# A Fourier layer and two gated blocks in one kernel: bias product on 128 rows, deferred threshold passes, and a later first inverse block

## The chip, the cores and the metric

The kernel runs on one core of one Trainium2 chip. The metric is the device time of one execution in microseconds (us). Three executions of the kernel before gave 1218.69, 1220.3 and 1221.24 us, median 1220.3. The engines are called PE (TensorE, the matrix engine), VectorE (DVE in the rows), ScalarE (ACT), GpSimd (POOL) and SyncE (SP, which only issues DMAs here). Each takes its own instructions in the order of the program and waits for the others by semaphores.

## What is computed

`x` has the shape 2 x 3008 x 256. The reference first applies a layer in the frequency domain, then two gated blocks on all 6016 tokens:

```python
X = np.fft.rfft(x, axis=1)
Yr = Xr @ w_r - Xi @ w_i + b_r
Yi = Xr @ w_i + Xi @ w_r + b_i
Yr = np.sign(Yr) * np.maximum(np.abs(Yr) - lam, 0.0)     # lam = 0.01, the same for Yi
y = np.fft.irfft(Yr + 1j * Yi, n=x.shape[1], axis=1)
h = y @ w_in;  x1 = (h * np.clip(h + 3.0, 0.0, 6.0) / 6.0) @ w_out       # d_ff 2048
out = (silu(x1 @ w_gate) * (x1 @ w_val)) @ w2_out                       # d_ff 1536
```

## The kernel before

**Layout of the transform.** 3008 is 47 x 64. The forward transform is done in two stages of matmuls, the inverse likewise. Frequencies are handled in 12 groups: 2 batches times 6 (`ORDER`, line 468), here called group 0 to 11. `pre` (line 309) is stage one on a slice of the input; its results go through DRAM (`Bd`) and come back transposed as `z`. Per group p:

- `s2` (line 384), stage two, called for two halves of the features. Eight PE matmul records each (L391). ScalarE copies one part of the result (L397) and rounds all of it to the high part of `X` (L398); VectorE forms a third combination, `sum` (L399), and the low part of `X` (L130). High and low part of the sum follow: a ScalarE cast (L404) and a VectorE subtraction (L130), both through the lists `later` and `last`.
- `ln` (line 421), the learned product with the complex weights in split precision, called for two halves h of the frequencies. One matmul of `ones` with `shift` adds the biases (L438): both tiles have 64 rows, of which rows 0 and 32 of `ones` are 1 and carry the high and the low part of the bias. 18 products follow (L433 to L435): 12 into bank `p`, on top of the bias, and 6 into bank `p1`. ScalarE copies `p1` (`k1`, L444), VectorE adds it to both halves of `p` (`yb`, L446), ScalarE takes a relu (`yc`, L448), VectorE a min and an addition (`yp`, L450): the last two are the threshold.
- `ia` (line 452), the first stage of the inverse: 16 PE records on half of the rows each (64 rows, `tile_position` 0 or 64, L459), two ScalarE copies (L462), and a DMA from GpSimd's queue to `Cd` in DRAM (L463).

`post` (line 544) is the second stage of the inverse for one block of 512 tokens and one half of the features: it needs `ct`, which `load_ct` (line 528) reads back from `Cd`, does 12 PE records (L541), a ScalarE cast to the high part `xa` (L552) and a VectorE subtraction for the low part (L130). The first block needs the groups 0 to 5 of batch 0 complete.

`unit` (line 618) is one step of the first gated block on the first tokens: one or two steps of weight conversion (`conv1.step`, line 197: four VectorE and two ScalarE instructions and a load `st`), `lower` (line 583, the split of the previous unit's result: a cast L579 and a subtraction L130), `project1` (line 555: six products, L125 to L127, then a relu L563 and a min and product L564), and `outp` (six products for each of two outputs). From group 8 on (`FROM`), units run between the pieces of the groups, and the last 4 groups thus share PE with them. Conversion steps run in `ln` for the groups 1 to 7.

**Order.** The order is written out by hand in the list `seq` (lines 488 to 504); each entry is called through `run` (line 411). For group p, `l` is the two halves of `ln`, `S(p + 1)` the two halves of the next group's stage two, `a` the inverse of the group before, `u` a unit from group 8 on:

```python
seq += l[:1] + u + some + S(p + 1)[:1] + u + S(p + 1)[1:] + a + u + l[1:] + u
seq += [sent]
...
if p == NQ:
    seq += [lambda: nc.sync.dma_start(inv2_sb, inv2), lambda: load_ct(blocks[0])]
if p == FROM - 1:
    seq += [lambda: few.__setitem__(0, True)]
    seq += [lambda: post(blocks[0], 0), lambda: post(blocks[0], 1)]
```

So `post` for the first block is issued between group 7 and group 8, and the load of its `ct` behind group 6. `run` puts the high sums of the step before ahead of a step and their low parts behind it. Two or three PSUM pools serve the matmuls: eight banks in turn up to group 7, five from then on (`few`). The tag `r` has three buffers, which `yb`, `yc` and the units' results share.

Behind the groups the remaining units, the first gated block and the second one follow (line 640 on); the diff does not touch them, except for the list that `run` and `unit` empty.

`prepare` (line 262) fills `ones` on GpSimd (L272 to L275) and the biases on VectorE and ScalarE (L291 to L294) while stage one runs.

Of the kernel before, what the change touches and what calls it, by code (L numbers as in the profile page):

```python
# [83 lines left out]
def fourier_moe_kernel(ctx: ExitStack, tc: tile.TileContext, x, lin, bias, w1, w2, fwd1, inv2, fwd2,  # L84
# [44 lines left out]
    def low(o, full, hi):  # L129
        nc.vector.tensor_tensor(out=o, in0=full, in1=hi.bitcast(F32), op=ALU.subtract)  # L130
# [92 lines left out]
    shift = ap_.tile([64, 2 * DIM], F32R, name="shift")  # L223
    ones = ap_.tile([64, 128], F32R, name="ones")
# [37 lines left out]
    def prepare():  # L262
# [8 lines left out]
        o = spread("o_st")[:64, :128]  # L271
# [3 lines left out]
        nc.gpsimd.tensor_copy(ones, o)  # L275
        w = [lin_st[:, k] for k in range(2)]
# [11 lines left out]
        def shifts(i):  # L288
            b = b_st[:64]
            if i == 0:  # L290
                nc.vector.tensor_scalar(b, b, LAM, None, op0=ALU.add)  # L291
                nc.scalar.copy(shift, b)
            else:
                low(shift[32:], b[32:], shift[32:])  # L294
# [8 lines left out]
    def spread(name):  # L303
        return xs_p.tile([128, 2 * DIM], F32, tag="r", name=name, bufs=3)
# [79 lines left out]
    def s2(b, Q, dh):  # L384
# [18 lines left out]
        def then():  # L403
            nc.scalar.copy(hi_s, both_)  # L404
            last.append(lambda: low(lo_s, both_, hi_s))
# [3 lines left out]
    later, last = [], []  # L409

    def run(f):

        for g in later:
            g()
        later.clear()
        f()
        for g in last:
            g()
        last.clear()

    def ln(b, Q, h):
# [3 lines left out]
        if 0 < ORDER.index((b, Q)) < FROM:  # L425
            conv1.step()
        xs = [t[:, :, :, h * 128 : (h + 1) * 128] for t in X[b, Q]]
# [20 lines left out]
        nc.scalar.activation(yc, yb, AF.Relu, bias=edges)  # L448
        yp[b, Q, h] = ap_.tile([128, 2, DIM], F32, tag="yp", name=f"yp{b}_{Q}_{h}", bufs=3)
        nc.vector.scalar_tensor_tensor(out=yp[b, Q, h], in0=yb, scalar=0.0, in1=yc, op0=ALU.min, op1=ALU.add)  # L450
# [40 lines left out]
    for p in range(len(ORDER)):  # L491
# [3 lines left out]
        seq += l[:1] + u + some + S(p + 1)[:1] + u + S(p + 1)[1:] + a + u + l[1:] + u  # L495
# [5 lines left out]
        if p == FROM - 1:  # L501
            seq += [lambda: few.__setitem__(0, True)]
            seq += [lambda: post(blocks[0], 0), lambda: post(blocks[0], 1)]
# [114 lines left out]
    def unit():  # L618
# [7 lines left out]
        if 0 <= n - 1 < len(units):  # L626
            lower(units[n - 1])
        if n < len(units):
            k, f = units[n]
            state[units[n]] = project1(k, f, ntok(k))  # L630
# [568 lines left out]
```

## Time and profile before

| | |
|---|---|
| median of three executions | 1220.3 us (1218.69 to 1221.24) |
| the profiled execution | 1220.05 us, span 1218.3 us |
| PE busy | 1204.9 us, 99% of the span |
| PE weight loads busy (beside the matmuls) | 1000.6 us, 82% |
| VectorE, ScalarE, GpSimd busy | 919.0 us (75%), 777.4 us (64%), 49.7 us (4%) |
| mean granted clock of PE | 0.996 of full speed |
| instructions | 16275 |

The page divides the span into 40 slices of 30.5 us and gives the busy share of each engine and the clock granted to PE in tenths. The ends of matmuls in the trace are modelled, so matmuls overlap in it, and an interval is best measured from start to start. An idle time with "<-" behind it names what ended it. A line number is that of the kernel; L130 is the helper that forms every low part, so its rows are told apart by tile names.

### The profile page before, as it was taken

Reading aid. Unit: us, or ns where it says so; the run is one execution under the profiler, and the core shown is the slowest. Engines: PE = TensorE matmul, PEld = TensorE weight load, DVE = VectorE, ACT = ScalarE, POOL = GpSimd, SP = SyncE. Lnnn points to the kernel's source line nnn. Section 1 sums busy time; section 2 is a strip of 40 time slices with the busy share of each in tenths; the row PEclk is TensorE's granted clock in tenths of the full one; section 3 lists DMA queues with packets and bytes.
Section 4 is the critical chain, followed back from the end, with each engine's and each line's share of the span. In section 5 each row is a group of like instructions: output and inputs, shape, how many; then the busy total and the mean of one; then the engine's idle time right before and its main releaser. Section 6 shows DMA issues by size and latency. Waiting matters only on the chain.

```text
span 1218.3 us, 16275 instructions
## 1 busy us (share of the span) xinstructions
PE 1204.9 (99%) x5770; PEld 1000.6 (82%) x5770; DVE 919.0 (75%) x1631; ACT 777.4 (64%) x1431; POOL 49.7 (4%) x77
## 2 busy tenths in 40 slices
PE   9998999999999999999999999999999999999998
PEld 3788787888888888888889888888888888888997
DVE  5676876798888988998988766766666766766665
ACT  3565665677777777777767655655655665655554
POOL 3000000800000000000000000000000000000000
PEclk9998999999999999999999999999999999999999
DMA  8875541774454563464362544644644644644551
GB/s 299 298 266 185 175 136 61 243 259 156 165 195 153 169 217 132 149 228 147 121 238 108 182 156 155 225 156 156 225 158 159 227 163 164 228 161 158 190 194 70
DMA packets 58450, 220.12 MB, mean 181 GB/s; under 512 B 5968, under 2 KB 17584, under 8 KB 46640
## 3 DMA queue, kind: packets, MB, share of 16 engines
q1 hardware_dynamic: 55728, 209.92, 49.3%
q0 software_dynamic: 2496, 9.05, 2.2%
q8 instruction: 45, 0.74, 0.2%
q14 instruction: 37, 0.30, 0.1%
q10 hardware_dynamic: 144, 0.11, 0.0%
HBM read 172.66 MB, written 46.40 MB: 180 GB/s over the span
## 4 chain that ended last, share of the span: by engine, by line
PE 88%; DVE 5%; ACT 2%; DMA 2%; issue 2%; SPq 0%; POOL 0%; DVEq 0%; ACTq 0%; POOLq 0%
PE acc L127 11%; PE acc L125 11%; PE acc L126 11%; PE P L901 8%; PE P L903 8%; PE P L902 8%; PE Tb L902 4%; PE Tb L901 4%; PE Tb L903 4%; PE p L541 3%; PE Q L902 2%; PE Q L901 2%; PE Q L903 2%; PE p L459 1%; PE p L324 1%
## 5 line engine op out<-in xcount | busy, mean ns | idle before, releaser
L957 ACT COPY hold<-P 128x512 f32<-128x512 f32 (+1 forms) x224 | 128.3, 573 | 77.0 <-PE P L903 76.9
L130 DVE TENSOR_TENSOR gated<-s,gated 128x512 fp32r<-128x512 f32 (+1 forms) x144 | 97.3, 676 | 50.2 <-ACT gated L1086 50.2
L579 ACT CAST gated<-r 128x512 fp32r<-128x512 f32 (+1 forms) x160 | 98.1, 613 | 54.7 <-DVE r L948 54.6
L130 DVE TENSOR_TENSOR gated<-r,gated 128x512 fp32r<-128x512 f32 (+1 forms) x160 | 107.8, 674 | 22.3 <-ACT gated L579 18.4
L952 DVE TENSOR_TENSOR hold<-Q,hold 128x512 f32<-128x512 f32 (+1 forms) x112 | 75.9, 678 | 64.5 <-PE Q L903 53.8
L125 PE MATMUL acc<-gated,w_o 128*128 128x512 f32 (+1 forms) x320 | 124.5, 389 | 0.0
L127 PE MATMUL acc<-gated,w_o 128*128 128x512 f32 (+1 forms) x320 | 123.2, 385 | 0.0
L126 PE MATMUL acc<-gated,w_o 128*128 128x512 f32 (+1 forms) x320 | 123.2, 385 | 0.0
L944 ACT ACTIVATE r<-hold,consts 128x512 f32<-128x512 f32 (+1 forms) x120 | 85.7, 714 | 40.9 <-DVE hold L952 40.0
L127 PE MATMUL acc<-gated,slot 128*128 128x512 f32 (+1 forms) x288 | 111.1, 386 | 0.0
L125 PE MATMUL acc<-gated,slot 128*128 128x512 f32 (+1 forms) x288 | 111.0, 385 | 0.1
L126 PE MATMUL acc<-gated,slot 128*128 128x512 f32 (+1 forms) x288 | 110.9, 385 | 0.0
L952 DVE TENSOR_TENSOR hold<-P,hold 128x512 f32<-128x512 f32 (+1 forms) x112 | 75.8, 677 | 40.0 <-PE P L903 40.0
L1126 ACT ACTIVATE s<-hold 128x512 f32<-128x512 f32 (+1 forms) x72 | 44.8, 623 | 85.6 <-DVE hold L952 85.6
L952 DVE TENSOR_TENSOR hold<-Tb,hold 128x512 f32<-128x512 f32 (+1 forms) x112 | 76.0, 678 | 25.8 <-PE Tb L903 18.8
L901 PE MATMUL P<-xo,slot 128*128 128x512 f32 (+1 forms) x240 | 92.3, 385 | 1.8 <-DVE hold L952 1.2
L903 PE MATMUL P<-xo,slot 128*128 128x512 f32 (+1 forms) x240 | 91.6, 382 | 0.0
L902 PE MATMUL P<-xo,slot 128*128 128x512 f32 (+1 forms) x240 | 91.5, 381 | 0.0
L948 DVE SCALAR_TENSOR_TENSOR r<-r,hold 128x512 f32<-128x512 f32 (+1 forms) x120 | 81.2, 677 | 13.3 <-ACT r L944 12.2
L1086 ACT CAST gated<-s 128x512 fp32r<-128x512 f32 (+1 forms) x144 | 88.0, 611 | 1.2 <-DVE s L1141 1.2
L1131 ACT ACTIVATE s<-hold 128x512 f32<-128x512 f32 (+1 forms) x72 | 45.0, 625 | 51.9 <-DVE hold L952 50.2
L127 PEld LDWEIGHTS acc<-gated,w_o 128*128 128x128 f32 x320 | 60.1, 188 | 11.3
(189 smaller groups left out, 2914.8 us busy)
## 6 DMA issues: line engine op xcount, KB each, us to landing
slot<-Wd SPq DMA_DIRECT2D x72, 1152.0 KB, 5.1
slot<-Sd SPq DMA_DIRECT2D x40, 896.0 KB, 4.8
st<-in_w SPq DMA_DIRECT2D x68, 256.0 KB, 4.9
Wd<-slot SPq DMA_DIRECT2D x12, 1152.0 KB, 5.1
z<-Bd SPq DMA_DIRECT2D x12, 512.0 KB, 5.3
Cd<-cs POOLq DMA_DIRECT2D x12, 512.0 KB, 4.7
Xd<-x SPq DMA_DIRECT2D x20, 256.0 KB, 2.3
raw<-Xd SPq DMA_DIRECT2D x5, 1024.0 KB, 7.4
```

The costliest lines, as they stand in the source:

```text
L125: nc.tensor.matmul(o, wl, xh, start=start, stop=False)
L126: nc.tensor.matmul(o, wh, xh, start=False, stop=False)
L127: nc.tensor.matmul(o, wh, xl, start=False, stop=stop)
L130: nc.vector.tensor_tensor(out=o, in0=full, in1=hi.bitcast(F32), op=ALU.subtract)
L579: nc.scalar.copy(hi[:, :n], g[:, :n])
L901: nc.tensor.matmul(o, wl, x[m][:, 0, :n], start=start, stop=False, skip_group_check=not start)
L902: nc.tensor.matmul(o, wh, x[m][:, 1, :n], start=False, stop=False, skip_group_check=not start)
L903: nc.tensor.matmul(o, wh, x[m][:, 0, :n], start=False, stop=True, skip_group_check=not start)
L944: nc.scalar.activation(r[:, :n], x[:, :n], AF.Relu, bias=three)
L952: nc.vector.tensor_tensor(out=h, in0=x[:, :n], in1=c, op=ALU.add)
L957: nc.scalar.copy(c, x[:, :n])
L1086: nc.scalar.copy(hi[:, :nb], t[:, :nb])
```

## The change

Four edits:

- `shift` and `ones` get 128 rows. The rows of `ones` but 0 and 32 stay zero, and rows 64 to 127 of `shift` are zeroed by a copy on GpSimd. The bias product thus runs on all 128 rows; the inverse (`ia`) keeps its 64-row form.
- `then` of `s2` issues the cast of the sum and the low part together. `ln` puts its relu and min into `later` as well. `run` hands the closures of the step before to `due`, and `flush` empties that list: behind the step, or inside it, in `ln` ahead of the products and in `unit` behind `lower`.
- `post` of the first block moves from the end of group 7 to behind the first half of `ln` of group 8, ahead of its first unit.
- In group 6 (`p == NQ`) the order becomes first half of `ln`, first half of stage two, inverse of group 5, second half of stage two, second half of `ln`.

```diff
@@ -220,8 +220,8 @@
     ap_ = pool(attn_stack, "attn", "right")
     linh = ap_.tile([128, 3, 2, DIM], F32R, name="linh")
     linl = ap_.tile([128, 3, 2, DIM], F32R, name="linl")
-    shift = ap_.tile([64, 2 * DIM], F32R, name="shift")
-    ones = ap_.tile([64, 128], F32R, name="ones")
+    shift = ap_.tile([128, 2 * DIM], F32R, name="shift")
+    ones = ap_.tile([128, 128], F32R, name="ones")
 
     NT = NJ // 4
     TC = 4 * DIM
@@ -268,11 +268,12 @@
             nc.gpsimd.memset(room[5][:, h * TC : (h + 1) * TC], 0.0)
         load_x(5)
         load_m(0, 0)
-        o = spread("o_st")[:64, :128]
+        o = spread("o_st")[:, :128]
         nc.gpsimd.memset(o, 0.0)
         for r in (0, 32):
             nc.gpsimd.memset(o[r : r + 1], 1.0)
         nc.gpsimd.tensor_copy(ones, o)
+        nc.gpsimd.tensor_copy(shift[64:], zeros[64:])
         w = [lin_st[:, k] for k in range(2)]
 
         def mixed(op):
@@ -289,9 +290,9 @@
             b = b_st[:64]
             if i == 0:
                 nc.vector.tensor_scalar(b, b, LAM, None, op0=ALU.add)
-                nc.scalar.copy(shift, b)
+                nc.scalar.copy(shift[:64], b)
             else:
-                low(shift[32:], b[32:], shift[32:])
+                low(shift[32:64], b[32:], shift[32:64])
 
         amid.update({
             6: [lambda: mixed(ALU.subtract), lambda: hi(2, 0)], 7: [lambda: mixed(ALU.add), lambda: hi(0, 2)],
@@ -402,21 +403,22 @@
 
         def then():
             nc.scalar.copy(hi_s, both_)
-            last.append(lambda: low(lo_s, both_, hi_s))
+            low(lo_s, both_, hi_s)
 
         later.append(then)
 
-    later, last = [], []
+    later, due = [], []
+
+    def flush():
+        while due:
+            due.pop(0)()
 
     def run(f):
 
-        for g in later:
-            g()
+        due.extend(later)
         later.clear()
         f()
-        for g in last:
-            g()
-        last.clear()
+        flush()
 
     def ln(b, Q, h):
 
@@ -424,6 +426,7 @@
             n_t[b, Q] = table("n", inv1, Q, f"n{b}_{Q}", 3)
         if 0 < ORDER.index((b, Q)) < FROM:
             conv1.step()
+        flush()
         xs = [t[:, :, :, h * 128 : (h + 1) * 128] for t in X[b, Q]]
 
         def product(o, form, k, start):
@@ -445,9 +448,13 @@
         yb = xs_p.tile([128, 2, DIM], F32, tag="r", name=f"yb{b}_{Q}_{h}", bufs=3)
         nc.vector.tensor_tensor(out=yb, in0=p, in1=k1.unsqueeze(1).to_broadcast([128, 2, DIM]), op=ALU.add)
         yc = xs_p.tile([128, 2, DIM], F32, tag="r", name=f"yc{b}_{Q}_{h}", bufs=3)
-        nc.scalar.activation(yc, yb, AF.Relu, bias=edges)
-        yp[b, Q, h] = ap_.tile([128, 2, DIM], F32, tag="yp", name=f"yp{b}_{Q}_{h}", bufs=3)
-        nc.vector.scalar_tensor_tensor(out=yp[b, Q, h], in0=yb, scalar=0.0, in1=yc, op0=ALU.min, op1=ALU.add)
+        y = yp[b, Q, h] = ap_.tile([128, 2, DIM], F32, tag="yp", name=f"yp{b}_{Q}_{h}", bufs=3)
+
+        def then():
+            nc.scalar.activation(yc, yb, AF.Relu, bias=edges)
+            nc.vector.scalar_tensor_tensor(out=y, in0=yb, scalar=0.0, in1=yc, op0=ALU.min, op1=ALU.add)
+
+        later.append(then)
 
     def ia(b, Q):
         c4 = ring4(f"cs{b}_{Q}")
@@ -492,7 +499,12 @@
         l, a = L(p), A(p - 1)
         some = [rest.pop(0) for _ in range(p in (1, 2))]
         u = [lambda: unit()] if p >= FROM else []
-        seq += l[:1] + u + some + S(p + 1)[:1] + u + S(p + 1)[1:] + a + u + l[1:] + u
+        head = l[:1] + ([lambda: post(blocks[0], 0), lambda: post(blocks[0], 1)] if p == FROM else [])
+        s = S(p + 1)
+        if p == NQ:
+            seq += head + s[:1] + a + s[1:] + l[1:]
+        else:
+            seq += head + u + some + s[:1] + u + s[1:] + a + u + l[1:] + u
         seq += [sent]
         if p in (2, 3):
             seq += [lambda i=p - 2: write_second(i)]
@@ -500,7 +512,6 @@
             seq += [lambda: nc.sync.dma_start(inv2_sb, inv2), lambda: load_ct(blocks[0])]
         if p == FROM - 1:
             seq += [lambda: few.__setitem__(0, True)]
-            seq += [lambda: post(blocks[0], 0), lambda: post(blocks[0], 1)]
     seq += [lambda: unit()] + A(len(ORDER) - 1)
 
 
@@ -625,6 +636,7 @@
                 conv1.step()
         if 0 <= n - 1 < len(units):
             lower(units[n - 1])
+        flush()
         if n < len(units):
             k, f = units[n]
             state[units[n]] = project1(k, f, ntok(k))
```

## Rows read from the trace of the kernel before

**Rows 1.** The page, busy tenths in 40 slices: PE and its granted clock.
```profile
PE   9998999999999999999999999999999999999998
PEclk9998999999999999999999999999999999999999
```
**Rows 2.** Stretches: length, busy us (count) by engine, granted clock, DMA share, GB/s.
```profile
63.07:65.75 2.68, 2.68 (x21) 2.44 (x21) 1.38 (x3) 1.42 (x3) 0.70 (x2) 1.00 0.77 231
91.12:101.10 9.98, 9.74 (x74) 8.34 (x72) 7.71 (x19) 6.54 (x17) 0.75 (x1) 1.00 0.59 188
99.46:103.07 3.61, 3.06 (x20) 2.55 (x20) 2.98 (x9) 3.11 (x9) 0.60 (x1) 1.00 0.03 9
108.00:112.35 4.35, 1.52 (x13) 1.34 (x12) 3.66 (x9) 3.37 (x10) 0.00 (x0) 0.94 0.86 227
117.60:122.20 4.60, 4.60 (x20) 4.17 (x20) 0.69 (x1) 0.58 (x1) 0.00 (x0) 0.52 0.07 27
```
**Rows 3.** Timeline of PE, groups 0 to 7: start, duration, instruction, idle before.
```profile
43.02 0.28 PE L434 MATMUL p<-linh,X 128*128 128x256 f32 x1
44.00 0.39 PE L435 MATMUL p<-linh,X 128*128 128x256 f32 x1 [0.70 <-DVE X L130]
...
45.94 1.95 PE L391 MATMUL p<-m,z 128*128 128x128 f32 x16
...
58.58 2.00 PE L459 MATMUL p<-yp,n 64*128 64x256 f32 x16
60.22 0.57 PE L438 MATMUL p<-shift,ones 64*128 64x512 f32 x1
...
60.95 0.28 PE L434 MATMUL p<-linh,X 128*128 128x256 f32 x1
...
62.86 0.28 PE L435 MATMUL p<-linh,X 128*128 128x256 f32 x1
...
63.72 0.28 PE L434 MATMUL p<-linh,X 128*128 128x256 f32 x1
63.84 0.28 PE L435 MATMUL p<-linh,X 128*128 128x256 f32 x1
...
94.96 2.00 PE L459 MATMUL p<-yp,n 64*128 64x256 f32 x16
...
112.35 5.32 PE L541 MATMUL p<-inv_sb,ct 96*128 96x94 f32 x24 [2.83 <-DMA ct<-Cd]
```
**Rows 4.** Timeline of PE: an inverse with full-row products behind it (group 9).
```profile
148.97 2.00 PE L459 MATMUL p<-yp,n 64*128 64x256 f32 x16
150.90 0.50 PE L125 MATMUL ph<-xa,w_g 128*128 128x512 f32 x1
151.24 0.40 PE L126 MATMUL ph<-xa,w_g 128*128 128x512 f32 x1
151.48 0.40 PE L127 MATMUL ph<-xa,w_g 128*128 128x512 f32 x1
```
**Rows 5.** Timelines of VectorE and of ScalarE in group 6.
```profile
97.93 0.69 DVE L450 SCALAR_TENSOR_TENSOR yp<-yb,yc 128x512 f32<-128x512 f32 x1 [0.79 <-ACT yc L448]
...
101.10 1.07 ACT L462 COPY cs<-p 128x512 f32<-128x512 f32 x2
```
**Rows 6.** Timeline of PE, groups 8 to 11.
```profile
128.05 1.99 PE L459 MATMUL p<-yp,n 64*128 64x256 f32 x14 [0.51 <-DVE r L564]
...
159.31 1.46 PE L541 MATMUL p<-inv_sb,ct 96*128 96x52 f32 x12
...
190.64 0.50 PE L125 MATMUL acc<-gs,w_o 128*128 128x512 f32 x1 [0.72 <-ACT gs L579]
```
**Rows 7.** Timelines of GpSimd and SP; the page's DMA issues, last number median landing.
```profile
14.73 0.51 POOL L331 DMA_DIRECT2D Bd<-first  x1 [4.47 <-DVE first L328]
...
38.72 0.38 SPq L380 DMA_DIRECT2D z<-Bd  x1
...
z<-Bd SPq DMA_DIRECT2D x12, 512.0 KB, 5.3
```

## Prediction

> **What bounds the kernel now.** I read the 40 slices of the page first. TensorE (PE) is at 90% or more in nearly every slice, and its clock has one dip behind the start, in the fourth slice [rows 1]. So the time is PE's work, plus the moments in which PE stands, plus what the lower clock costs. The diff reorders only the first 210 us; what follows keeps its instructions and their order and should move as a block.
>
> The table of stretches [rows 2] compares one piece of work. The 19 matmuls of the first half of `ln` (the bias product L438, then 18 products) take 2.68 us in group 3, 3.61 in group 7, and 4.60 in group 8, where the granted clock is 0.52, the lower of the two levels (1.2 GHz) nearly throughout. From 108.00 to 112.35 PE is busy for 1.52 us of 4.35. PE's timeline says why: it waits 0.70 us for `X` at 44.00, and 2.83 us for the transfer of `ct` at 112.35 [rows 3].
>
> VectorE and ScalarE cause both. In group 6 they need 9.98 us from one inverse's copies to the next, VectorE busy for 7.71 of it [rows 2], while PE's own pitch is 9.1 us (58.58 to 94.96, four groups, [rows 3]). VectorE's idle part stands above all in front of L450, 0.79 us each time, waiting for the relu issued just ahead of it [rows 5]. They fall nearly 0.9 us behind per group: the inverse of group 5 starts on PE at 94.96 [rows 3], its copies on ScalarE only at 101.10 [rows 5], 6.14 us later. The way from these copies through Cd and `ct` to L541 ends at 112.35, another 11.25 us.
>
> **The bias product on 128 rows.** From the last full-row product (62.86) to the second product behind the bias (63.72) is 0.86 us [rows 3]. With full rows I expect the pitches of ordinary neighbours: 0.12 (63.72 to 63.84), then 0.24 for 512 columns (151.24 to 151.48, [rows 4]), then 0.12: 0.48. Saved: 0.38. That holds for 17 of the 24 products: 12 first halves, and the second halves of groups 0 and 8 to 11, which no inverse precedes directly. 17 x 0.38 = 6.5 us.
>
> The second halves of groups 1 to 7 come behind the half-row inverse (in group 6 half of stage two now lies between; I count it alike). Before, from the first inverse matmul to the second product: 58.58 to 60.95 = 2.37 us [rows 3]. After, the switch of row modes lies ahead of the bias, as it does ahead of L125: 148.97 to 151.24 = 2.27 [rows 4], plus 0.12 = 2.39. So 7 x 0.02 = 0.1 is lost. The Trainium skill (TensorE: Matmul & The Clock Gate, Why this matters for your kernels) speaks against the change here: matmuls of few rows on different row groups run at the same time, and few rows take no less time than many. By that rule alone these seven lose their overlap with the inverse, 0.29 us each (L438 starts 1.64 us behind the first inverse matmul, L125 1.93), and the sum is 2 us smaller; the rows show the 0.29 come back at the exit. Between 0.1 and 2.0 I take 0.1, since both ends of it are measured.
>
> Group 0's first half gains little, since stage two behind it wants a `z` that lands about then: 0.1 off. The product's sum: **6.3 us**. The larger `ones` and the zeroing of 64 x 512 run on GpSimd, which is idle for 4.47 us ahead of its next DMA [rows 7]: 0 on the path, and above nothing only if they took longer than that, when the first Bd write would start as much later.
>
> **Threshold and sum passes a step later.** In a first half the relu and min now come behind stage two's first half, and the sums' high and low parts go together one step later. No instruction is added and no DMA moves with them. The stall ahead of L450 goes in first halves. Up to group 7 second halves keep it, because `sent` follows and flushes at once; and the last low sum now waits for the inverse's copies ahead of it on ScalarE (an estimate of 0.6, from two copies of 1.07 together, [rows 5]). VectorE's group becomes at most 7.7 + 0.8 + 0.6 = 9.1 us, PE's 9.1 - 0.4 = 8.7. It falls behind by 0.2 to 0.4 a group, 1 to 2 us by group 7. Two waits for `X` go: 43.02 to 44.00 in group 0, 0.98 - 0.12 = 0.86 [rows 3], and 3.61 - 2.68 = 0.93 in group 7 [rows 2]. **1.8 us.** What is late next is `z` of group 2: issued at 38.72 and landing 5.3 us later, at 44.0 [rows 7]; its stage two stands at 45.94 [rows 3] and moves up by 1.7. It just fits.
>
> In groups 8 to 11 the split of the previous unit now comes ahead of the relu and min. PE stood there 0.51 us for `r` at 128.05 and 0.72 for `gs` at 190.64 [rows 6]; by starts some 0.16 more each (0.86 against 0.70 at 44.00), so 1.5, and there may be shorter breaks which the view does not mark. The passes take 0.79 + 0.69 = 1.5 us out of the way [rows 5], more than either. I take **2.0** (0 to 3). `yp` comes later by some 3 us, but the inverse that reads it is a group behind.
>
> **First block a group later, inverse of group 5 earlier.** Nothing is added: 24 matmuls, two casts and two subtractions move behind the first half of group 8. The `ct` load keeps its place on SP; the tables, `st` and `z` queued behind it go out earlier with it. In group 6 the second half of stage two (half of 1.95 us, [rows 3]) moves behind the inverse, which so starts at about 94.96 - 1.0 - 3.5 (seven savings of 0.38 and the 0.86) = 90.5. With a lag of 1.5 to 3 us in place of 6.14 its copies begin by 93.5, and 11.25 later, by 104.8, `ct` is there. PE wants it at 109.5 (112.35 less the wait) - 4.8 + 2.3 = 107. So the wait goes: 2.83 + 0.16 = **3.0 us**.
>
> With it goes the lower clock. The 24 L541 took 5.32 us [rows 3] against 2 x 1.46 [rows 6], the first half of group 8 4.60 against 2.68 [rows 2]: 2.4 + 1.9 = **4.3 us**. A stand of 0.72 at 190.64 has left no mark in the slices of the clock.
>
> Given back: the split of the block stood behind 4.60 us of products; now the first unit wants it at once. With VectorE 1 to 2 us behind, I put this at **1.0** (0 to 3, the wait that it replaces).
>
> **Sum.** 6.3 + 1.8 + 2.0 + 3.0 + 4.3 - 1.0 = 16.4 us. The profiled execution took 1220.05 (span 1218.3), 0.25 under the median of 1220.3; so 1203.65 on its own scale, 1203.9 on the median's.
>
> **Rivals.** (a) The wait for `ct` stays, or one as long for the block's split takes its place, and the clock falls again. It decides if ScalarE is over 5 us late at the inverse of group 5 (90.5 + 5 + 11.25 = 107). For: it was 6.14. Against: the order takes out the stalls that made it so. Loses 3.0 + 4.3: 1211.2. The Trainium skill (the same page and section) warns of idle gaps in mid-kernel that bring the clock down; the dip behind the wait for `ct` agrees.
> (b) VectorE, not PE, sets the pace of groups 1 to 7. PE's savings there (7 x 0.38), the 0.93 and 2 more of the block's split are lost, 5.6 in all: 1209.5. For: 9.1 against 8.7 is close, and the other way round. Against: that deficit is first stored in PE's lead, which reached 6.14 us before it cost 0.93.
> (c) The bias product does not do what it says, because the gap behind it comes from adding to the bank just written. Then the 6.3 become about 0: 1210.2. Against: L125 opens another bank, and 0.34 follows it all the same behind the inverse [rows 4]; products that add to one bank follow at 0.12 [rows 3].
> (d) The overlap of row groups counts in full: 1205.9.
> (e) Slower: the wait ahead of the first block stays, and the clock, once down, stays down. Before, 9.9 us at the lower level (5.32 + 4.60) cost 4.3. Without the 7.3 of wait and clock the change gains 9.1, so it decides at some 21 us more at that level, all of group 8 and half of group 9; at 30 more (13 us) it is 1224. Against: the clock came back within group 8 while PE worked without a break, and nothing there takes that away.
>
> **Chances.** Forecast 0.60; (a) 0.14; (b) 0.09; (c) 0.07; (d) 0.04; (e) 0.06. About 0.2% (2.4 us) can be told from no change. All but (e) are faster by more than that; for two of (a) to (c) falling together I leave some to no change: faster 0.90, same 0.04, slower 0.06. The forecast's own ends are 1200 (nothing given back, 3 us in the units, some on PE's other switches) and 1207; with (a) to (d) the range is 1200 to 1211.5.
>
> **What would show it.** Right: L433 within 0.25 us of L438, and 2.3 us for the 19 matmuls; no wait for `ct`; granted clock 1.00 from 100 to 210; the copies of group 5 within 3 us of their inverse; no PE wait for `X`. Wrong: PE standing over 2 us anywhere between 100 and 115, a digit under 9 in the clock's slices behind the start, L433 still 0.4 us behind L438, or waits of PE for VectorE in groups 1 to 8.

## The result, and the profile after

Four executions of the kernel after took 1200.01 to 1204.32 us, median 1200.66; four of the kernel before, beside them, had the median 1220.72. The ratio is 0.9845, 95% interval [0.9822, 0.9868]: 20 us faster. The forecast was 1203.9, its range 1200 to 1211.5; the result lies just inside the lower end. The profiled execution took 1200.14 us, its span is 1198.4.

The page of the kernel after, PE and its clock in 40 slices. The dip of [rows 1] is gone.

```profile
PE   9999999999999999999999999999999999999998
PEclk9999999999999999999999999999999999999999
```

The waits of PE up to 210 us, kernel after: total, times, longest. No row for `ct`, `X`, `r` or `gs` is left. What stands is the wait at the very start, which was there before, and two short ones for `z`.

```profile
PE p L259 <- DVE zeros L142: 1.5, 1, 1.5
PE p L392 <- issue: 0.5, 1, 0.5
PE p L392 <- DMA z<-Bd: 0.3, 1, 0.3
```

The timeline of PE, kernel after. L441 is the bias product (L438 before), L436 to L438 the products, L466 the inverse, L552 the first block (L541 before), L125 to L127 the units.

```profile
46.17 2.00 PE L466 MATMUL p<-yp,n 64*128 64x256 f32 x16
48.10 0.50 PE L441 MATMUL p<-shift,ones 128*128 128x512 f32 x1
48.44 0.28 PE L436 MATMUL p<-linl,X 128*128 128x256 f32 x1
48.55 0.28 PE L437 MATMUL p<-linh,X 128*128 128x256 f32 x1
...
60.87 0.28 PE L438 MATMUL p<-linh,X 128*128 128x256 f32 x1
60.99 0.40 PE L441 MATMUL p<-shift,ones 128*128 128x512 f32 x1
61.23 0.28 PE L436 MATMUL p<-linl,X 128*128 128x256 f32 x1
61.34 0.28 PE L437 MATMUL p<-linh,X 128*128 128x256 f32 x1
...
90.45 2.00 PE L466 MATMUL p<-yp,n 64*128 64x256 f32 x16
...
106.85 2.77 PE L552 MATMUL p<-inv_sb,ct 96*128 96x94 f32 x24
109.45 0.47 PE L125 MATMUL ph<-xa,w_c 128*128 128x512 f32 x1
...
110.64 0.40 PE L126 MATMUL ph<-xa,w_c 128*128 128x512 f32 x1
111.03 0.50 PE L127 MATMUL ph<-xa,w_c 128*128 128x512 f32 x1
...
173.00 0.39 PE L125 MATMUL acc<-gs,w_o 128*128 128x512 f32 x1
173.23 0.39 PE L126 MATMUL acc<-gs,w_o 128*128 128x512 f32 x1
173.45 0.39 PE L127 MATMUL acc<-gs,w_o 128*128 128x512 f32 x1
```

Read it against [rows 3]. From the last full-row product to the second one behind the bias: 60.87 to 61.34 = 0.47 us, before 0.86. Behind the inverse: 46.17 to 48.55 = 2.38, before 2.37. The inverse of group 5 starts at 90.45 instead of 94.96. The 24 matmuls of the first block begin at 106.85 with no wait, and the next product starts at 109.45: 2.60 us from start to start, where before it was 5.25 (112.35 to 117.60) behind a wait of 2.83. Of the products at 173.00, the first waited 0.72 for `gs` before [rows 6], and now waits for nothing.

The timeline of VectorE in group 6, kernel after. In the first half, two passes (L400, L130) stand between `yb` (L449) and the min (L455), which thus finds its relu done. In the second half the stall of [rows 5] remains, at 98.61.

```profile
90.98 0.68 DVE L449 TENSOR_TENSOR yb<-p,k 128x512 f32<-128x512 f32 x1
91.58 0.42 DVE L400 TENSOR_TENSOR sum<-p,sum 128x256 f32<-128x256 f32 x1
91.91 0.68 DVE L130 TENSOR_TENSOR X<-p,X 128x512 fp32r<-128x512 f32 x1
92.50 0.68 DVE L455 SCALAR_TENSOR_TENSOR yp<-yb,yc 128x512 f32<-128x512 f32 x1
...
98.61 0.69 DVE L455 SCALAR_TENSOR_TENSOR yp<-yb,yc 128x512 f32<-128x512 f32 x1 [0.79 <-ACT yc L454]
```

ScalarE, kernel after: the copies of group 5 (L469, in [rows 5] at 101.10), then the two casts of the block's split (L563) with the deferred relu between them.

```profile
92.48 1.07 ACT L469 COPY cs<-p 128x512 f32<-128x512 f32 x2
...
108.32 0.59 ACT L563 CAST xa<-p 128x512 fp32r<-128x512 f32 x1 [0.83 <-PE p L552]
108.80 0.72 ACT L454 ACTIVATE yc<-yb,consts 128x512 f32<-128x512 f32 x1
109.66 0.59 ACT L563 CAST xa<-p 128x512 fp32r<-128x512 f32 x1
```

The copies come 92.48 - 90.45 = 2.03 us behind the start of their inverse; before it was 6.14.

Stretches of the kernel after: PE is busy throughout, at a clock of 1.00. In [rows 2], PE worked 1.52 us of the 4.35 that ended with the wait, and the clock then fell to 0.52.

```profile
90.00:110.00 20.00, 20.00 (x164) 18.56 (x162) 16.76 (x39) 13.94 (x34) 1.51 (x2) 1.00 0.74 243
110.00:130.00 20.00, 20.00 (x121) 16.84 (x120) 18.79 (x49) 14.37 (x36) 0.75 (x1) 1.00 0.58 188
```

**Where the 19.9 us of span came from**, by the starts of the same work in both timelines of PE:

| point | before | after | gained by here | forecast by here |
|---|---|---|---|---|
| end of stage two and products of group 0 | 44.22 | 42.57 | 1.65 | 1.5 |
| end of the products of group 7 | 109.36 | 104.46 | 4.90 | 5.0 |
| first product of the first unit | 122.20 | 109.45 | 12.75 | 12.7 |
| first unit product behind the last inverse | 207.67 | 189.14 | 18.53 | 16.4 |
| first product behind the units that waits for `hold` (L901, after L913) | 275.66 | 257.12 | 18.54 | 16.4 |
| span | 1218.3 | 1198.4 | 19.9 | 16.4 |

The forecast's 1.0 given back at the block's split is counted behind the point of the first unit's first product.

### The profile page after: what moved, and what is told of

It is laid out like the page before. It is cut to its first block, busy times and chain, and to the rows that moved or that the text cites. A ratio compares the mean times of both kernels' runs of the same rounds, so it can differ in the third digit from the quotient of the medians.

```text
span 1198.4 us, 16285 instructions
## 1 busy us (share of the span) xinstructions
PE 1191.2 (99%) x5770; PEld 996.4 (83%) x5770; DVE 919.2 (77%) x1631; ACT 778.5 (65%) x1431; POOL 50.4 (4%) x78
## 4 chain that ended last, share of the span: by engine, by line
PE 95%; DVE 2%; ACT 1%; DMA 1%; issue 1%; DVEq 0%; ACTq 0%
PE acc L125 12%; PE acc L127 12%; PE acc L126 12%; PE P L913 8%; PE P L915 8%; PE P L914 8%; PE Tb L915 4%; PE Tb L913 4%; PE Tb L914 4%; PE p L552 2%; PE Q L915 2%; PE Q L913 2%; PE Q L914 2%; PE p L466 2%; PE p L392 2%; PE p L437 1%
## 5 line engine op out<-in xcount | busy, mean ns | idle before, releaser
L130 DVE TENSOR_TENSOR gated<-s,gated 128x512 fp32r<-128x512 f32 (+1 forms) x144 | 97.4, 676 | 50.2 <-ACT gated L1098 50.1
L130 DVE TENSOR_TENSOR gated<-r,gated 128x512 fp32r<-128x512 f32 (+1 forms) x160 | 107.9, 675 | 22.4 <-ACT gated L590 18.5
L125 PE MATMUL acc<-gated,w_o 128*128 128x512 f32 (+1 forms) x320 | 124.5, 389 | 0.0
L127 PE MATMUL acc<-gated,w_o 128*128 128x512 f32 (+1 forms) x320 | 123.2, 385 | 0.0
L127 PE MATMUL acc<-gated,slot 128*128 128x512 f32 (+1 forms) x288 | 111.1, 386 | 0.0
L125 PE MATMUL acc<-gated,slot 128*128 128x512 f32 (+1 forms) x288 | 111.0, 385 | 0.1
L913 PE MATMUL P<-xo,slot 128*128 128x512 f32 (+1 forms) x240 | 92.2, 384 | 0.6 <-DVE hold L964 0.5
L127 PEld LDWEIGHTS acc<-gated,w_o 128*128 128x128 f32 x320 | 60.1, 188 | 11.2
```

What stands on the lines that cost most here:

```text
L125: nc.tensor.matmul(o, wl, xh, start=start, stop=False)
L127: nc.tensor.matmul(o, wh, xl, start=False, stop=stop)
L913: nc.tensor.matmul(o, wl, x[m][:, 0, :n], start=start, stop=False, skip_group_check=not start)
```

## The experiments

The forecast by points is good, but it credits each part with a share: bias product 6.3, deferral 1.8 + 2.0, the later block (with the new order of group 6) 3.0 + 4.3 - 1.0. The trace of the kernel after can't show whether these shares are right, since all parts act at once. So each part was taken out alone, and each was put in alone. "To before" is the ratio to executions of the kernel before on the same chip.

| run | kernel | median us (range) | to before [95%] |
|---|---|---|---|
| a_bias64 | after, bias on 64 rows | 1207.42 (1207.04 to 1209.55) | 0.9902 [0.9888, 0.9917] |
| a_inline | after, no deferral | 1212.7 (1210.85 to 1214.24) | 0.9939 [0.9925, 0.9954] |
| a_post_early | after, block early | 1201.24 (1199.69 to 1201.79) | 0.9846 [0.9832, 0.9860] |
| a_order6 | after, old order in group 6 | 1201.67 (1201.02 to 1202.93) | 0.9853 [0.9839, 0.9867] |
| b_defer | before, with the deferral | 1207.49 (1206.64 to 1207.84) | 0.9901 [0.9883, 0.9918] |
| b_post | before, with the later block | 1215.31 (1213.89 to 1217.28) | 0.9966 [0.9956, 0.9976] |
| b_bias | before, bias on 128 rows | 1216.0 (1210.45 to 1217.34) | 0.9973 [0.9962, 0.9984] |
| b_bias_again | the same, another trace | 1213.4 (one execution) | (1218.57 beside it) |
| a_thr_inline | after, only the sums deferred | 1208.65 (1207.53 to 1210.2) | 0.9912 [0.9895, 0.9928] |
| a_sum_inline | after, only the threshold deferred | 1201.44 (1200.91 to 1202.11) | 0.9852 [0.9837, 0.9867] |
| merged | after, two inverses together | 1204.92 (1202.1 to 1205.56) | 0.9877 [0.9857, 0.9896] |
| after_again | after | 1201.22 (1200.89 to 1202.28) | 0.9852 [0.9834, 0.9870] |

The kernel after has two medians, 1200.66 and 1201.22; differences from it are given against both.

### One part taken out

**a_bias64.** The bias product back on 64 rows, the rest as after.

```diff
-    shift = ap_.tile([128, 2 * DIM], F32R, name="shift")
-    ones = ap_.tile([128, 128], F32R, name="ones")
+    shift = ap_.tile([64, 2 * DIM], F32R, name="shift")
+    ones = ap_.tile([64, 128], F32R, name="ones")
...
```

> The changed kernel with the bias product back on 64 rows; the deferral, the later first block and the order of group 6 stay. My theory (the switch of row modes costs 0.38 us at each of 17 bias products and nothing at the other 7): 6.4 us above the changed kernel's 1200.7, so 1207.1 (1206 to 1208); a first half of ln takes 2.68 us again against 2.39, and 0.86 us instead of 0.47 lie between the last full-row product ahead of the bias and the second product behind it. Rival (the gap came from adding to the bank just written, or from waits that the deferral took out): 1200.7 to 1202.

6.2 to 6.8 us slower than after. Up to 210 us its only waits, beside the one at the very start, are 0.7 and 0.5 for `z`, and its clock is 1.00. From the last full-row product to the second one behind the bias it is 0.85 us again (62.60 to 63.45). So the bias product's own step accounts for the loss, and it is worth about its 6.3 here. If adding to a bank just written made the gap (rival (c)), this change would have cost nothing.

**a_inline.** Without the deferral: `run`, the relu and min, and the sums as before.

```diff
...
-        due.extend(later)
+        for g in later:
+            g()
         later.clear()
         f()
-        flush()
+        for g in last:
+            g()
+        last.clear()
...
-        def then():
-            nc.scalar.activation(yc, yb, AF.Relu, bias=edges)
-            nc.vector.scalar_tensor_tensor(out=y, in0=yb, scalar=0.0, in1=yc, op0=ALU.min, op1=ALU.add)
-
-        later.append(then)
+        nc.scalar.activation(yc, yb, AF.Relu, bias=edges)
+        nc.vector.scalar_tensor_tensor(out=y, in0=yb, scalar=0.0, in1=yc, op0=ALU.min, op1=ALU.add)
...
```

> The changed kernel without the deferral: relu and min again straight behind the addition, high sums ahead of a step and low sums behind it. My theory (the parts hang together; without the deferral VectorE and ScalarE set the pace of groups 3 to 7, so that PE's savings there are lost in waits for X and the block's split stands late): 10 to 13 us above the changed kernel, 1211 to 1214, waits of PE for X in groups 5 to 7, ScalarE's copies of group 5 at least 4 us behind their inverse, and short breaks for gs and r in groups 8 to 11. Rival (the parts add up and the deferral is worth its own 1.8 and 2.0 to 2.8): 1204.5 to 1205.3.

11.5 to 12.0 us slower. The waits of PE up to 210 us in this kernel (L434 to L436 are the products):

```profile
PE p L436 <- DVE X L130: 4.2, 5, 1.9
...
PE p L434 <- ACT X L399: 1.0, 2, 0.7
PE acc L125 <- ACT gs L584: 0.7, 1, 0.7
```

PE waits for `X`, 5.2 us in all. The copies of group 5 start 5.4 us behind the start of their inverse (98.84 against 93.45), and the block's matmuls 7.5 us later than after (114.33 against 106.85). They do not wait for `ct`, which the later block leaves time for, and the clock is 1.00 from 100 to 135 us: here the lateness shows in the waits for `X`. This is rival (b): without the deferral, VectorE and ScalarE set the pace.

**a_post_early.** The block back between groups 7 and 8, the rest as after.

```diff
-        head = l[:1] + ([lambda: post(blocks[0], 0), lambda: post(blocks[0], 1)] if p == FROM else [])
...
             seq += [lambda: few.__setitem__(0, True)]
+            seq += [lambda: post(blocks[0], 0), lambda: post(blocks[0], 1)]
```

> The changed kernel with the first block's inverse back between groups 7 and 8; deferral, 128 rows and the order of group 6 stay. My theory (the wait for ct came from ScalarE's lag; with the lag gone ct lands at about 102, and PE asks for it only at 104.5): no wait for ct, granted clock 1.00 from 90 to 130, and a time within 0.7 us of the changed kernel, 1200 to 1201.4, since the move is then worth nothing. Rival (the move itself took out the wait and the low clock, 3.0 and 4.3 us): 1208, with a wait of 2 to 3 us at L541 and a clock near 0.5 behind it.

0.0 to 0.6 us from after: no difference. PE's timeline shows the block's matmuls 3.56 us earlier than after, and still nothing waits:

```profile
103.29 2.77 PE L552 MATMUL p<-inv_sb,ct 96*128 96x94 f32 x24
105.89 0.48 PE L441 MATMUL p<-shift,ones 128*128 128x512 f32 x1
```

So with the other three parts in place, the move of the block is worth nothing that can be told. What took the wait away is that the copies are no longer late.

**a_order6.** The old order in group 6, the rest as after.

```diff
-        s = S(p + 1)
-        if p == NQ:
-            seq += head + s[:1] + a + s[1:] + l[1:]
-        else:
-            seq += head + u + some + s[:1] + u + s[1:] + a + u + l[1:] + u
+        seq += head + u + some + S(p + 1)[:1] + u + S(p + 1)[1:] + a + u + l[1:] + u
```

> The changed kernel with the old order in group 6 (the inverse of group 5 behind both halves of stage two). My theory: ct lands some 1 to 2 us later, at about 103 to 104, still ahead of PE, which asks for it at 106.9: no change, within 0.5 us of 1200.7. Rival (the earlier inverse is what brings ct in time): a wait at L541 of 0.5 us or more, 1201.5 to 1206.

0.4 to 1.0 us above after, a little over what was expected of the theory. The block's matmuls wait for nothing, so the rival's mechanism did not occur. PE's timeline of this kernel has a wait that after lacks, about a group ahead of the edit:

```profile
81.70 0.57 PE L392 MATMUL p<-m,z 128*128 128x128 f32 x3 [0.50 <-DMA z<-Bd]
```

Waits for `z` of 0.3 to 0.8 us come and go in these traces, in after too. Whether the order of group 6 is worth anything can't be told.

### One part put in alone

**b_defer.** The kernel before with the deferral: `run`, `flush` and `then` of the diff, without its other hunks.

```diff
...
-        for g in later:
-            g()
+        due.extend(later)
         later.clear()
         f()
-        for g in last:
-            g()
-        last.clear()
+        flush()
...
```

> The kernel before with the deferral alone (threshold and sum passes a step later; bias on 64 rows, first block between groups 7 and 8, old order in group 6). My theory (the deferral alone takes away ScalarE's lag, and with it the waits for X, the wait for ct, the low clock and the short breaks of groups 8 to 11): 10 to 13 us below the kernel before, clock 1.00 throughout, ct landing within half a microsecond of PE's asking for it. Rival (the parts add up, and the deferral has only its own 1.8 and 2.0 to 2.8): 3.8 to 4.6 us below, with the wait for ct and the low clock still there.

11.8 us faster than before. PE's timeline, inverse of group 5 and first block:

```profile
94.66 2.00 PE L465 MATMUL p<-yp,n 64*128 64x256 f32 x16
...
108.12 2.77 PE L547 MATMUL p<-inv_sb,ct 96*128 96x94 f32 x24
```

ScalarE's timeline, the copies of group 5:

```profile
96.69 1.07 ACT L468 COPY cs<-p 128x512 f32<-128x512 f32 x2 [0.23 <-PE p L465]
```

Block early, group 6 in its old order, bias on 64 rows, and yet the copies follow their inverse after 2.03 us, the block starts without a wait, and the clock is 1.00 from 100 to 130. The load of `ct`, issued at 101.37, lands 5.4 us later, some 1.3 us ahead of the block, where half a microsecond was expected. The deferral alone does what the prediction booked under four terms: waits for `X` 1.8, units, wait 3.0, clock 4.3.

**b_post.** The kernel before with the block later.

```diff
-        seq += l[:1] + u + some + S(p + 1)[:1] + u + S(p + 1)[1:] + a + u + l[1:] + u
+        head = l[:1] + ([lambda: post(blocks[0], 0), lambda: post(blocks[0], 1)] if p == FROM else [])
+        seq += head + u + some + S(p + 1)[:1] + u + S(p + 1)[1:] + a + u + l[1:] + u
...
-            seq += [lambda: post(blocks[0], 0), lambda: post(blocks[0], 1)]
```

> The kernel before with the first block's inverse moved behind the first half of group 8, and nothing else. My theory (ScalarE and VectorE are still some 4.5 us behind there, so the wait turns up again at the block's split, with xa instead of ct): 4 to 6 us below the kernel before, PE standing 1.5 to 3 us at the first unit's products or at the split's bank, no wait for ct above 0.5 us. Rival (the wait and the low clock are both gone for good): 7.3 us below.

3.9 us faster than before. PE's timeline:

```profile
112.58 2.77 PE L541 MATMUL p<-inv_sb,ct 96*128 96x94 f32 x24
116.71 0.51 PE L125 MATMUL ph<-xa,w_c 128*128 128x512 f32 x1 [1.36 <-ACT xa L552]
```

Its stretch behind that wait, with a granted clock of 0.71:

```profile
115.00:120.00 5.00, 3.64 (x13) 2.58 (x13) 4.21 (x11) 3.30 (x8) 0.00 (x0) 0.71 0.66 248
```

The wait for `ct` is gone, but as long as VectorE and ScalarE are late, half of it comes back as a wait for the block's split: rival (a) in its second form. PE's waits for `X` also rise, from 1.3 us in two to 2.1 in three, and the gain stays a little under the 4 to 6 us that were expected.

**b_bias** and **b_bias_again.** The kernel before with the bias product on 128 rows.

```diff
-    shift = ap_.tile([64, 2 * DIM], F32R, name="shift")
-    ones = ap_.tile([64, 128], F32R, name="ones")
+    shift = ap_.tile([128, 2 * DIM], F32R, name="shift")
+    ones = ap_.tile([128, 128], F32R, name="ones")
...
```

> The kernel before with the bias product on 128 rows, and nothing else. My theory (VectorE and ScalarE set the pace of groups 3 to 7 there, so that PE's savings turn into longer waits for X and ct, and only those of groups 8 to 11 and of the first groups come through): 2.5 to 4.5 us below the kernel before, PE waiting over 4 us in all for X and ct against 4.1 before, and the low clock still there. Rival (the savings come through wherever they are made): 6.4 us below.

3.5 us faster than before by the medians, about half of the 6.3. The profiled execution was the fastest of twelve; eleven lie at 1214.6 to 1217.3. Its waits of PE for `X` rose from 1.3 us in two ([rows 3] has the first) to 2.8 in six, and its clock never fell, which does not fit the others. So the same kernel was looked at again:

> The kernel before with the bias on 128 rows, once more, for a second trace: one execution of it was profiled at 1210.45 us with the clock at 1.00 throughout, eleven others took 1214.6 to 1217.3. My theory (what differs is whether the clock falls behind the same wait for ct): a profiled time of 1215 to 1217 with the granted clock near 0.5 for some 10 us behind L541, the waits for X and ct within 1 us of the first trace. Rival (what differs are the waits themselves): waits for X, ct or z longer by 4 us or more, and the clock at 1.00.

This execution took 1213.4 us, less than the 1215 to 1217 expected; its span is 1211.6. The first block and the stretch behind it in both, first b_bias (timeline of PE):

```profile
111.24 2.85 PE L542 MATMUL p<-inv_sb,ct 96*128 96x94 f32 x24 [1.65 <-DMA ct<-Cd]
```

b_bias, stretch:

```profile
115.00:120.00 5.00, 5.00 (x33) 4.53 (x33) 3.80 (x9) 2.34 (x6) 0.00 (x0) 1.00 0.40 157
```

b_bias_again, timeline of PE:

```profile
111.77 3.71 PE L542 MATMUL p<-inv_sb,ct 96*128 96x94 f32 x24 [2.19 <-ACT cs L463]
```

b_bias_again, stretch:

```profile
115.00:120.00 5.00, 5.00 (x23) 4.90 (x23) 1.66 (x3) 0.77 (x3) 0.00 (x0) 0.50 0.45 175
```

The second row names the copies (L463) as the releaser, those of group 6, which start at 111.15. But in b_bias the block starts at 111.24 while the same copies (from 111.16, 1.07 us) still run, so PE does not need them; the load of `ct`, issued at 106.86 in b_bias_again, landed 4.8 us later, at about 111.66, and is what it waited for. With 1.65 us of standing the clock stayed up, with 2.19 it fell to the lower level. The first unit starts at 116.38 in the one and at 119.69 in the other: 3.3 us, 0.5 of it the block's later start, so the low clock cost 2.8. The spans differ by 2.9 (1208.7 and 1211.6). The eleven other executions lie 4.1 to 6.9 us above the first one, with a mean granted clock of 0.995 to 0.997 against its 0.999, which fits a fall of the clock in them too; without traces of them, the rest of the difference stays open.

The 3.5 is thus, as far as this shows, what the change is worth where the clock falls as before. Up to the first block the savings are lost: PE asks for `ct` at 111.24 - 1.65 = 109.6, no earlier than before (109.5), though nine bias products had been shortened by then. Its marked waits up to there grew by 1.5 us for `X`, and by 1.1 for `z` in the first trace.

a_inline and b_post differ by the bias product and the order of group 6. They are 2.6 us apart (3.3 by their ratios to before), so without the deferral the bias product is worth about half there too.

### The deferral cut in two

**a_thr_inline.** After, with the relu and min issued at once, and the sums still deferred.

```diff
-        def then():
-            nc.scalar.activation(yc, yb, AF.Relu, bias=edges)
-            nc.vector.scalar_tensor_tensor(out=y, in0=yb, scalar=0.0, in1=yc, op0=ALU.min, op1=ALU.add)
-
-        later.append(then)
+        nc.scalar.activation(yc, yb, AF.Relu, bias=edges)
+        nc.vector.scalar_tensor_tensor(out=y, in0=yb, scalar=0.0, in1=yc, op0=ALU.min, op1=ALU.add)
```

> The changed kernel with relu and min back behind the addition (inline), the sums' passes still deferred. My theory (the stall of 0.79 ahead of the min, once per first half, is what makes VectorE's group longer than PE's 8.7 us): 5 to 11 us above the changed kernel, PE waits for X in groups 5 to 7 and short breaks for gs and r in groups 8 to 11. Rival (the sums' order is what counts): within 2 us of the changed kernel.

7.4 to 8.0 us slower than after. ScalarE's timeline shows how a relu issued early hurts what stands behind it:

```profile
111.03 0.72 ACT L451 ACTIVATE yc<-yb,consts 128x512 f32<-128x512 f32 x1 [1.10 <-DVE yb L449]
111.66 1.05 ACT L559 CAST xa<-p 128x512 fp32r<-128x512 f32 x2
```

And PE's timeline who pays for it:

```profile
108.00 2.77 PE L548 MATMUL p<-inv_sb,ct 96*128 96x94 f32 x24
112.28 0.50 PE L125 MATMUL ph<-xa,w_c 128*128 128x512 f32 x1 [1.51 <-ACT xa L559]
```

The relu waits for a `yb` that VectorE has not made yet, the casts of `xa` wait in line behind it, and PE waits for `xa`. In the next stretches the clock is 0.79 (110 to 115) and 0.87 (115 to 120).

**a_sum_inline.** After, with the sums' high and low parts as before, and the threshold still deferred.

```diff
-            low(lo_s, both_, hi_s)
+            last.append(lambda: low(lo_s, both_, hi_s))
 
-        later.append(then)
+        ahead_of.append(then)
...
+        for g in ahead_of:
+            g()
+        ahead_of.clear()
         due.extend(later)
         later.clear()
         f()
         flush()
+        for g in last:
+            g()
+        last.clear()
```

> The changed kernel with the sums' passes back as before (high sum ahead of a step, low sum behind it), relu and min still deferred. My theory (a stall of 0.64 a group comes back in one place and one of 0.6 goes in another; the wait in group 0 comes back): 0 to 2 us above the changed kernel. Rival (the sums' order is what counts): 6 us or more above it, with waits for X.

0.2 to 0.8 us above after, within the scatter of the two. With the threshold passes deferred, the order of the sums is worth nothing that can be told. With them inline it is worth something: a_inline, with both back, takes 4.0 us more than a_thr_inline by the medians, 3.3 by the ratios to before. So of the deferral's 11.5 to 12.0 us the threshold passes alone decide over 7.4 to 8.0, and the rest is lost only when both are back. The threshold's deferral alone in the kernel before was not run.

### A step further

**merged.** Fewer switches between row modes: the inverses of two groups one behind the other, every second group (`yp` gets a fourth buffer for it, taken when its min is issued).

```diff
...
-        l, a = L(p), A(p - 1)
+        l, a = L(p), []
...
-        head = l[:1] + ([lambda: post(blocks[0], 0), lambda: post(blocks[0], 1)] if p == FROM else [])
+        head = l[:1] + (A(p - 2) + A(p - 1) if p % 2 == 0 else []) + ([lambda: post(blocks[0], 0), lambda: post(blocks[0], 1)] if p == FROM else [])
...
```

> The changed kernel with the first stage of the inverse run for two groups in one go, behind the first half of ln of every second group (and both last ones at the end), with four buffers for its input and that tile taken when the min is issued. Six of the twelve switches into and out of the half-row form go. My theory (a pair of switches costs some 0.3 to 0.4 us wherever PE sets the pace): 1.8 to 2.4 us below the changed kernel run beside it, with no new wait. Rival (two inverses at once bring four copies at once on ScalarE and a wait for them or for yp): as fast as the changed kernel or up to 3 us slower, with a wait of PE for yp or for the copies.

A miss: 3.7 us slower than after_again, beside it on the chip. PE's timeline has four new waits for `X`, two in the first half of group 6 and two in that of group 8; one of each:

```profile
85.54 0.38 PE L438 MATMUL p<-linh,X 128*128 128x256 f32 x1 [0.55 <-DVE X L130]
...
104.10 0.38 PE L438 MATMUL p<-linh,X 128*128 128x256 f32 x1 [0.55 <-DVE X L130]
```

From the start of the first stage two to the first half of group 5 it did gain 0.6 us (48.36 against 48.97), 0.3 for each of the two pairs of switches gone by then. But in the odd groups the inverse had stood behind stage two, ahead of the products of the second half, and had covered VectorE's way to the next group's `X`. With the inverse moved away, the products of the even groups come to `X` too early. The four waits are 1.5 us together, and two more in the units, for `gs`, are 0.5; where the rest of the 3.7 lies was not followed up.

**after_again.** The kernel after once more, as the measure of the runs above.

> The changed kernel once more, beside the merged inverse and the bias alone: 1200 to 1202.5, and 18 to 20 us below the kernel before.

1201.22 us, waits for `z` of 0.4 and 0.4, clock 1.00. None of the runs is better than the kernel after by more than they scatter.

## Why the prediction was right, point by point

**Bias product: 6.3 forecast, 6.2 to 6.8 measured (a_bias64).** The steps hold: 0.47 us where 0.48 was forecast, 2.38 behind the inverse where 2.39 was. The Trainium skill (TensorE: Matmul & The Clock Gate, Why this matters for your kernels) has few-row matmuls on different row groups run at the same time, from which rival (d) took 2 us. The rows show that overlap before (L438 started 1.64 us behind the first inverse matmul, L441 does so after 1.93), but the 2.37 before and 2.38 after show that nothing was lost with it. Rival (c) falls with a_bias64 and with the 0.47. The sum counts the 6.3 without a condition; only rival (b) has them depend on VectorE keeping up. They do: alone they are 3.5 (b_bias).

**Waits for `X`: 1.8 forecast, gone.** The stall ahead of the min is gone in first halves and stays in second ones, as the step on the deferral had it. PE's group is 8.70 us (65.26 to 73.96, the inverses of two neighbours), forecast 8.7. The lag of 2.03 us lies in the forecast 1.5 to 3. The gain up to group 7 came out at 4.90 against 5.0.

**`z` of group 2 "just fits": it did.** Its stage two starts at 44.29 with no wait. The two waits for `z`, 0.51 us at 29.47 (counted as issue; 0.30 before) and 0.35 at 35.94, are those of groups 0 and 1. The second one takes the saving in the first half of group 0, as the prediction said, only whole: the stage two behind it starts at 35.94, before at 35.87.

**Units: 2.0 forecast (0 to 3), about 3.6 measured.** This term was mis-sized, and its own range missed. By starts, five breaks of before are gone: 1.2 ahead of the inverse at 128.05, 0.5 and 0.5 around the output products at 146.96 and 169.24, 1.0 and 0.4 at 190.64 and 191.50. The view of waits marks only the first and the fourth, 2.2 together where 1.5 was booked; the prediction named shorter breaks as possible and gave them 0.5, where they were 1.4.

**Wait for `ct` 3.0 and low clock 4.3: both gone, but for a reason placed wrongly.** The step "First block a group later, inverse of group 5 earlier" counted the wait out by all three changes at once: PE asks later, the inverse comes earlier, the lag is shorter. Its arithmetic gave `ct` at 104.8 and PE at 107. In the trace PE asks at 106.85; the load is issued at 97.15 and takes 4.8 us, so `ct` is there at about 101.95: the copies start at 92.48, and the way from them took 9.5 us, not 11.25. But this booked 7.3 us under the move, and a_post_early and b_defer show that they belong to the deferral: it is enough without the move, and the move without it (b_post) keeps a wait of 1.36 and part of the low clock, and gains 3.9 where 7.3 were booked. The sentence on rival (a), that "the order takes out the stalls that made it so", was the right reason. That the sum came out all the same is partly luck: since all edits were made together, it did not matter under which of them the 7.3 stood. Read for the deferral alone, the same working gives 3.8, and b_defer measured 11.8. The Trainium skill (the same page and section) warns of idle gaps in mid-kernel that bring the clock down; the runs agree for 2.19 us in b_bias_again, and show no fall for 1.65 in b_bias and 1.93 in a_inline.

**Given back: 1.0 forecast (0 to 3), 0.5 measured.** The second cast of the block's split stands behind the deferred relu on ScalarE (108.80, then 109.66). The first unit's first six products take 1.91 us from start to start (109.45 to 111.36), before 1.39 (122.20 to 123.59); the longest step is the one to L127 at 111.03, 0.39 where 0.23 is usual.

**The sum.** At the last inverse 18.5 were gained where 16.4 were forecast: 1.6 more in the units, 0.5 less given back, and 0.1 more in the bias products of groups 8 to 11 (0.40 each), less the 0.1 up to group 7. Another 1.4 us of the span lie behind the part that the diff reorders, where PE's waits for `hold` are 1.7 us before (from 275.66 on) and 0.5 after. The instructions there are the same. In after_again, the same kernel as after, these waits are 1.9 us and the span is 1200.5 instead of 1198.4; so this part of the gain comes and goes from one execution to the next, and the change can't be credited with it.

| part | forecast | taken out of after | alone in before |
|---|---|---|---|
| bias product | 6.3 | 6.2 to 6.8 | 3.5 |
| deferral | 1.8 + 2.0 | 11.5 to 12.0 | 11.8 |
| block later, without group 6 | 3.0 + 4.3 - 1.0, with group 6 | 0.0 to 0.6 | 3.9 |
| order of group 6 | (in the line above) | 0.4 to 1.0 | not run |

The two columns of runs each add up to about 20 only by chance: alone, the deferral and the later block both act on the same wait, so each is credited with part of its 7.3 us; and the bias product needs the deferral to be worth all of its 6.3.

**Rivals.** (a) and (b) did not come about in the kernel after, but both are real: each shows where the deferral is left out ((a) in b_post, (b) in a_inline). (e) had the clock stay down behind a wait; in every run where it fell it was back at 1.00 in the stretch from 125 to 130 us.

## What to carry to other kernels

Where two engines pass work to and fro in order, follow how late each has become by the end of the stage, and not the busy share: 0.8 us of VectorE waiting for a relu issued just ahead of its min, twice in each group, was the main part of what led to a 7.3 us loss on PE half a dozen groups later. Put other work between a producer's instruction and its consumer's, and look at what stands in line behind an instruction that waits. When several edits bear on one wait, take each out and put each in alone before the gain is credited to any: here one cured it without the others, another was worth its full price only beside that one, and the two halves of the deferral did not add up either.

## What was not expected of the hardware

The clock's answer to a stand of PE is not a matter of its length alone in these runs: 1.65 us in b_bias and 1.93 in a_inline, with full-pace work behind them, left 1.00; 1.36 in b_post and 1.51 in a_thr_inline, each with short breaks among the unit's products right behind it, were followed by stretches of 5 us at 0.71 and at 0.79, and 2.19 in b_bias_again by one at 0.50. PE's timeline in a_inline, and the stretch that holds the wait, with a granted clock of 1.00:

```profile
105.41 0.39 PE L436 MATMUL p<-linh,X 128*128 128x256 f32 x1 [1.93 <-DVE X L130]
```

```profile
100.00:115.00 15.00, 11.79 (x92) 10.71 (x93) 11.23 (x27) 9.64 (x24) 1.51 (x2) 1.00 0.68 224
```

One kernel can fall on either side: the two traces of b_bias differ by the 2.8 us of the low clock.

64 more rows of zeros made the step over the bias product 0.39 us shorter (0.86 to 0.47), where its neighbours have full rows on both sides. Behind a half-row inverse the same rows changed nothing (2.37 and 2.38). This points to the step from one row mode to the other and back as the cost, not to the number of rows; merged, with two pairs of such steps fewer up to group 5, gained 0.3 us for each. The Trainium skill (TensorEngine Tiling (Array Packing), Key Properties) says that a change of tiling mode drains the engine; the rows fit that, and give the pair of changes 0.39 us.
